# An RWKV6 and MoE kernel on one core: DMA transposes in place of PE transposes for k, r and the MoE input, and a longer lag of the second matmul

## The chip, the cores and the metric

The kernel runs on one core of one Trainium2 chip. The metric is device time in microseconds (us) of one execution. Every timed comparison uses runs of the two kernels on the same chip in the same rounds. A run counts as "slow" when it is more than 1.5% above the fastest run of the same kernel, and ratios use the other, fast runs alone.

The engines are named as in the profile: PE is the matmul engine and PEld its weight loads, DVE, ACT and POOL are the vector, scalar and general-purpose engines, and SP is the engine whose queue starts all DMAs of this kernel.

## The reference

Attention in the RWKV6 form, then a two-layer MoE block with a tanh gelu. Sizes: 4 batches, 8 heads, 768 steps, head width 48; model width 384, hidden width 2048.

```python
def _attn_ref(r, k, v, w, u):            # each [B, H, S, D] = [4, 8, 768, 48]
    state = zeros(B, H, D, D)
    for t in range(S):
        cur = einsum('bhd,bhe->bhde', u * k[t], v[t])
        y[t] = einsum('bhd,bhde->bhe', r[t], state + cur)
        state = w[t][..., None] * state + einsum('bhd,bhe->bhde', k[t], v[t])
    return y

x = attn_out.transpose(0, 2, 1, 3).reshape(B * S, H * D)      # [3072, 384]
h = x @ w_in                                                  # [3072, 2048]
g = 0.5 * h * (1 + tanh(sqrt(2/pi) * (h + 0.044715 * h**3)))
out = g @ w_out                                               # [3072, 384]
```

## The kernel before

The work is cut into 12 units: 3 windows of 256 steps, 4 batches each. A turn of the main loop does the MoE of unit q, the attention matmuls of unit q+1, and the decays and multiplies ("prep") of unit q+2. The matmuls take k and r (already multiplied by decays, called kk and rq) and the attention output x with another axis on the partitions, so the PE transposes them itself, into PSUM (in the trace of before 0.90 us per unit for k and r and 0.33 for x), and DVE copies the result out (0.68 us each for k and r, 0.56 for x).

```python
    # prep(q): products on DVE, one instruction per tensor
    DVE.tensor_tensor(out=kk[:, :, :, 0:D], in0=tdh(kt), in1=dec(e1), op=AL.mult)
    DVE.tensor_tensor(out=rq[:, :, :, 0:D], in0=tdh(rt), in1=dec(fq), op=AL.mult)

    def a2(q, which):                       # transposes of k (0) and r (1)
        src = (kk, rq)[which]
        ps = ps_a.tile([P, G, 2, 2, 64], BF, tag="a", name=f"T{q}_{which}")
        for g in range(G):
            for t2 in range(2):
                PE.transpose(ps[:, g, :, t2, :], src[:, t2, ds(2 * g, 2), :], ident)
        dst = pw2.tile([P, G, 2, 2, 64], BF, tag=f"T{which}", name=f"TT{q}_{which}")
        DVE.tensor_copy(out=dst, in_=ps)

    # a3(q, rnd): the score matmuls "mt", stationary kT = TT_0, moving rT = TT_1
    # a5(q, c2):  y += rT x state on PE, then ACT copies y to xs[:, c2, :]

    def a6(q):                              # transpose of x
        for c2 in range(2):
            for cb in range(NCB):
                PE.transpose(ps[:, cb, c2, :], xs[:, c2, ts(cb, P)], ident)
        DVE.tensor_copy(out=xT, in_=ps.rearrange("p a b t -> p a (b t)"))

    # mm1(q, i): six matmuls into PSUM tile h (two buffers), then one gelu on ACT
    # mm2(q, c2, fts): one matmul per ft into o (c2 is the half of the 256 rows)

    for q in range(NU):
        # ... loads of k, r, v (unit q+3) and w (unit q+4) ...
        table("gelu")                       # ACT table load
        ramp = q < 2                        # ... ramp: all mm1 first ...
        for i in range(8):
            if not ramp:
                mm1(q, i)
            if i >= 2:                      # mm2 lags mm1 by two
                mm2(q, 0, (2 * i - 4, 2 * i - 3))
            if i in (1, 3, 4, 5, 6, 7):
                next(att, None)             # a2 | a3 | a3 | a4 | a5 | a5 of unit q+1
            # ... cumulative sums of unit q+2 at i == 6 ...
        table("exp")                        # ACT table load
        exps(q + 2); ln(q + 3)              # decays, on ACT
        mm2(q, 0, range(12, 16))
        # ... a6(q + 1) ...
        store(q, 0)                         # DVE copy, two DMAs
        prep(q + 2); prep_b(q + 2)
        mm2(q, 1, range(16))
        store(q, 1)
```

## Time and profile before

| | before |
|---|---|
| median (3 runs), us | 235.33 (235.24 to 236.41) |
| span of the profiled run, us | 235.9 |
| granted PE clock, mean | 0.968 |
| period of a unit in the steady part, us | 16.56 |
| first mm1 of unit 2 (third unit) / of unit 11 (last), us | 74.04 / 220.64 |

To see what sets the period of a unit, one boundary between two units has to be read on two engines. This is the PE timeline of before: start, time, engine, line, operation, output and inputs, sizes, number of instructions and, in brackets, an idle time ahead of them with what ended it.

```profile
136.21 0.82 PE L345 MATMUL h_7_2167<-xT_1899,w_in_sb 128*128 128x256 bf16 x6
...
138.10 0.49 PE L329 MATMUL xTp_2196<-ident,xs_2148 128*128 128x128 bf16 x6
138.43 2.76 PE L354 MATMUL o_1_2223<-w_out_sb,g_1948 128*128 128x384 bf16 x16
141.03 0.82 PE L345 MATMUL h_0_2253<-xT_2203,w_in_sb 128*128 128x256 bf16 x6
141.69 0.82 PE L345 MATMUL h_1_2261<-xT_2203,w_in_sb 128*128 128x256 bf16 x6
142.34 0.61 PE L236 MATMUL T_1_2269<-ident,rq_128 128*128 128x128 bf16 x8
142.79 0.61 PE L236 MATMUL T_0_2280<-ident,kk_126 128*128 128x128 bf16 x8
143.75 0.81 PE L345 MATMUL h_2_2291<-xT_2203,w_in_sb 128*128 128x256 bf16 x6 [0.36 <-ACT g_2252 L347]
```

And this is the ACT timeline of before over the same stretch.

```profile
137.06 0.60 ACT L347 ACTIVATE g_1948<-h_7_2167 128x512 bf16<-128x512 f32 x1 [1.75 <-PE h_7_2167 L345]
137.56 0.49 ACT L321 ACTIVATE xs_2148<-y_1_2071 128x384 bf16<-128x384 f32 x1
138.06 1.28 ACT L156 ACT_TABLE_LOAD   x1
...
141.81 1.28 ACT L158 ACT_TABLE_LOAD   x1
143.10 0.60 ACT L347 ACTIVATE g_2252<-h_0_2253 128x512 bf16<-128x512 f32 x1
```

From the last gelu of a unit (137.06) to the first of the next (143.10) ACT has 6.04 us of work without a gap: the copy of xs, two table loads, the decays. The PE has only two PSUM buffers for h, so h_2 can't start before that gelu has read h_0; it waits 0.36 us. Everything that the PE does between h_7 and h_2, the transposes included, therefore lies in the shadow of this ACT chain. A unit is this shadow plus the PE work from h_2 to the end of h_7 (9.67 us).

The stores are the only DMAs of before that are as small as the new transposes. From the SP timeline of before (four stores issued in 4.87 us, some of that waiting for data) and from its list of DMA issues (count, KB each, median us from issue to landing):

```profile
123.12 4.87 SPq L365 DMA_DIRECT2D out_dram<-ob_1901  x4
128.09 0.55 SPq L69 DMA_DIRECT2D k_1939<-in_k_dram  x1
```

```profile
out_dram<-ob_1901 SPq DMA_DIRECT2D x4, 96.0 KB, 2.2
```

The load of k takes SP 0.55 us to issue (those of r, v and w behind it 0.68, 0.86 and 1.17), a store 0.55 to 0.58 where two follow each other without a wait (1.12 and 1.10 us for two); a store lands in 2.2 us from the start of its issue.

### The profile page before, as it was taken

The page shows a single profiled execution, that of the slowest core. Times are in us where ns is not written, and L with a number is a line of the kernel's source. Part 1 is how long each engine was busy: PE and PEld are TensorE (multiplying, and loading weights), DVE is VectorE, ACT ScalarE, POOL GpSimd, SP SyncE. Part 2 cuts the span into 40 slices and gives each one's busy share as a digit, 9 for nine tenths or more (in the row PEclk, how much of TensorE's full clock was granted, in tenths as well). Part 3 has the DMA queues.
Part 4 walks back from the last instruction along what each step waited for, and adds up shares of the span by engine and source line. Part 5 has one row for each costly group of instructions (what it writes and reads, how often), then busy time and mean ns, then how long its engine had stood idle before and what let it go on. Part 6 is the DMA issues. An engine that isn't in the chain of part 4 may idle for free.

```text
span 235.9 us, 5759 instructions
## 1 busy us (share of the span) xinstructions
PE 203.4 (86%) x2448; PEld 143.0 (61%) x2448; DVE 131.3 (56%) x211; ACT 134.0 (57%) x223; POOL 104.5 (44%) x87
## 2 busy tenths in 40 slices
PE   0456787598895999999999999999999999999992
PEld 0334564357564767667767667676777677677761
DVE  7684686561636538547547747656285376374200
ACT  3433780566255449459368377395494684765670
POOL 3473792639008504806708509329158076060000
PEclk9999996779997999999999999999999999999998
DMA  7999999713902911942923914915719120020202
GB/s 173 307 396 297 331 320 255 160 33 72 231 15 54 246 25 36 206 98 53 232 56 75 257 24 111 210 33 124 182 35 212 24 62 10 13 56 0 68 1 67
DMA packets 56969, 30.45 MB, mean 129 GB/s; under 512 B 50928, under 2 KB 56176, under 8 KB 56944
## 3 DMA queue, kind: packets, MB, share of 16 engines
q1 hardware_dynamic: 56944, 30.09, 52.1%
q8 instruction: 19, 0.31, 0.6%
q14 instruction: 6, 0.05, 0.1%
HBM read 25.36 MB, written 4.72 MB: 127 GB/s over the span
## 4 chain that ended last, share of the span: by engine, by line
PE 54%; ACT 19%; DVE 11%; issue 9%; POOL 3%; DMA 2%; DVEq 0%; ACTq 0%; POOLq 0%
ACT L156 5%; DVE w_out_sb L86 2%; DMA w_89<-in_w_dram 2%; PE o_0_532 L354 1%; DVE rq_127 L203 1%; ACT logw_124 L162 1%; PE o_0_3678 L354 1%; PE o_0_3457 L354 1%; PE o_0_3175 L354 1%; PE o_1_3740 L354 1%; PE o_1_3632 L354 1%; PE o_1_3389 L354 1%; POOL rk_418 L210 1%; POOL rk_418 L212 1%; ACT logw_122 L162 1%
## 5 line engine op out<-in xcount | busy, mean ns | idle before, releaser
L345 PEld LDWEIGHTS <-w_in_sb 128*128 128x128 bf16 x576 | 54.0, 99 | 21.1 <-issue 9.9
L156 ACT ACT_TABLE_LOAD x13 | 16.7, 1283 | 0.9 <-PEq L487 0.7
L158 ACT ACT_TABLE_LOAD x12 | 15.4, 1283 | 0.2
L171 PEld LDWEIGHTS <-strict 128*128 128x128 bf16 x24 | 2.5, 104 | 9.9 <-issue 9.5
L215 POOL TENSOR_TENSOR am_997<-blk,al_975 128x384 f32<-128x384 bf16 x2 | 2.4, 1230 | 12.5 <-ACT al_975 L187 12.5
L215 POOL TENSOR_TENSOR am_1304<-blk,al_1273 128x384 f32<-128x384 bf16 x2 | 2.4, 1229 | 11.5 <-ACT al_1273 L187 11.5
L215 POOL TENSOR_TENSOR am_1608<-blk,al_1577 128x384 f32<-128x384 bf16 x2 | 2.4, 1230 | 8.3 <-ACT al_1577 L187 8.3
L215 POOL TENSOR_TENSOR am_1912<-blk,al_1881 128x384 f32<-128x384 bf16 x2 | 2.4, 1230 | 8.3 <-ACT al_1881 L187 8.3
L215 POOL TENSOR_TENSOR am_2216<-blk,al_2185 128x384 f32<-128x384 bf16 x2 | 2.4, 1230 | 8.3 <-ACT al_2185 L187 8.3
L215 POOL TENSOR_TENSOR am_2520<-blk,al_2489 128x384 f32<-128x384 bf16 x2 | 2.4, 1228 | 8.3 <-ACT al_2489 L187 8.3
L215 POOL TENSOR_TENSOR am_2811<-blk,al_2780 128x384 f32<-128x384 bf16 x2 | 2.4, 1228 | 7.9 <-ACT al_2780 L187 7.9
L215 POOL TENSOR_TENSOR am_3100<-blk,al_3069 128x384 f32<-128x384 bf16 x2 | 2.4, 1228 | 7.9 <-ACT al_3069 L187 7.9
L215 POOL TENSOR_TENSOR am_3382<-blk,al_3352 128x384 f32<-128x384 bf16 x2 | 2.4, 1228 | 7.9 <-ACT al_3352 L187 7.9
L354 PE MATMUL o_0_532<-w_out_sb,g_437 128*128 128x384 bf16 x16 | 5.5, 469 | 0.2 <-ACT w_out_sb L84 0.2
L236 PEld LDWEIGHTS <-rq_127 128*128 128x128 bf16 x48 | 3.4, 104 | 3.3 <-DVE rq_127 L203 3.2
L354 PEld LDWEIGHTS <-g_437 128*128 128x128 bf16 x32 | 3.3, 117 | 3.2 <-issue 2.5
L170 PE MATMUL cum_0_201<-logw_122,strict 128*128 128x384 bf16 x1 | 0.5, 479 | 5.4 <-ACT logw_122 L162 5.4
L362 DVE COPY ob_3736<-o_0_3678 128x384 f32<-128x384 f32 x1 | 0.6, 558 | 7.7 <-PE o_0_3678 L354 7.7
L215 POOL TENSOR_TENSOR am_699<-blk,al_677 128x384 f32<-128x384 bf16 x2 | 2.3, 1187 | 4.3 <-ACT al_677 L187 4.3
L354 PEld LDWEIGHTS <-g_3653 128*128 128x128 bf16 x32 | 3.0, 98 | 1.7 <-ACT g_3653 L347 0.4
L238 DVE COPY TT_1_818<-T_1_809 128x1024 bf16<-128x1024 bf16 x1 | 0.7, 692 | 6.0 <-PE T_1_809 L236 6.0
L354 PE MATMUL o_0_3678<-w_out_sb,g_3653 128*128 128x384 bf16 x16 | 3.8, 327 | 0.0
(942 smaller groups left out, 694.2 us busy)
## 6 DMA issues: line engine op xcount, KB each, us to landing
wi_155<-in_moe_w_in_dram SPq DMA_DIRECT2D x1, 512.0 KB, 5.0
wi_157<-in_moe_w_in_dram SPq DMA_DIRECT2D x1, 512.0 KB, 6.0
wi_159<-in_moe_w_in_dram SPq DMA_DIRECT2D x1, 512.0 KB, 6.7
wi_161<-in_moe_w_in_dram SPq DMA_DIRECT2D x1, 512.0 KB, 7.5
wi_163<-in_moe_w_in_dram SPq DMA_DIRECT2D x1, 512.0 KB, 8.7
wi_165<-in_moe_w_in_dram SPq DMA_DIRECT2D x1, 512.0 KB, 9.6
w_89<-in_w_dram SPq DMA_DIRECT2D x1, 384.0 KB, 3.7
k_91<-in_k_dram SPq DMA_DIRECT2D x1, 384.0 KB, 4.7
```

What stands on the lines that cost most here:

```text
L86: eng.tensor_copy(out=out, in_=in_)
L156: ACT.preload_act_table_set(EXP_SET)
L158: ACT.preload_act_table(AF.Gelu_apprx_tanh)
L162: ACT.activation(out=lw[:, :, :, 0:D].rearrange("p t h d -> p h t d"), in_=ld.pop(("w", q)).rearrange("p h (t d) -> p h t d", t=2), func=A ...
L171: PE.matmul(dst[:, 0:HD], s1, lw[:, 1, :, 0:D], start=False, stop=True)
L203: DVE.tensor_tensor(out=rq[:, :, :, 0:D], in0=tdh(rt), in1=dec(fq), op=AL.mult)
L210: POOL.tensor_tensor(out=rk, in0=kt.rearrange("p h (t d) -> p h t d", t=2), in1=rt.rearrange("p h (t d) -> p h t d", t=2), op=AL.mult)
L212: POOL.tensor_tensor(out=rk, in0=rk, in1=u_bc[:, :, None, :].broadcast_to([P, H, 2, D]), op=AL.mult)
L215: POOL.tensor_tensor(out=am[:, c2], in0=blk.rearrange("p g j d -> p g (j d)"), in1=al[:, :, c2][:, :, None].broadcast_to([P, G, 2 * D]), o ...
L236: PE.transpose(ps[:, g, :, t2, :], src[:, t2, ds(2 * g, 2), :], ident)
L345: PE.matmul(h[:, f, :], w_in_sb[:, cb, ts(ft, P)], xT[:, cb, :], start=(f + cb == 0), stop=(cb == NCB - 1), skip_group_check=True)
L354: PE.matmul(st["o", q, c2], g[:, ft, ts(c2, P)], w_out_sb[:, ft, :], start=(ft == 0), stop=(ft == NFT - 1))
```

## The change

Its intent is to take the transposes off the PE, and their copies out of PSUM off DVE, from the third unit on: SP starts DMAs that transpose from SBUF to SBUF. k and r get two each (64 rows of 1024 elements, so that each half has the layout that the matmuls need), x gets one. They are started as soon as kk and rq are multiplied, at the end of a turn of the loop; before transposes the same unit's k and r behind h_1 of the next turn. The multiplies are halved (one per t2) for the new layout; mm2 lags mm1 by four groups in place of two, and the scores move one group earlier. In the ramp, the second unit's x is now transposed ahead of the multiplies on DVE.

```diff
     def a2(q, which):
-        src = (kk, rq)[which]
-        ps = ps_a.tile([P, G, 2, 2, 64], BF, tag="a", name=f"T{q}_{which}")
-        for g in range(G):
-            for t2 in range(2):
-                PE.transpose(ps[:, g, :, t2, :], src[:, t2, ds(2 * g, 2), :], ident)
-        dst = pw2.tile([P, G, 2, 2, 64], BF, tag=f"T{which}", name=f"TT{q}_{which}")
-        DVE.tensor_copy(out=dst, in_=ps)
+        src = (kk_ps, rq_ps)[which][q % 2]
+        dst = pw2.tile([P, 2, G, 2, 64], BF, tag=f"T{which}", name=f"TT{q}_{which}")
+        if q < 2:
+            ...                              # on the PE, as before
+            return
+        for c2 in range(2):
+            SP.dma_start(out=dst[:, c2].rearrange("p g t x -> p (g t) x"),
+                         in_=src[ds(64 * c2, 64)].rearrange("p g t j d -> p (g t j d)"),
+                         transpose=True)
@@ a6
+        if q < 2:
+            ...                              # on the PE, as before
+        else:
+            SP.dma_start(out=xT.rearrange("p a b t -> p (a b) t"),
+                         in_=xs.rearrange("p a c -> p (a c)"), transpose=True)
@@ main loop
-            if i >= 2:
-                mm2(q, 0, (2 * i - 4, 2 * i - 3))
-            if i in (1, 3, 4, 5, 6, 7):
+            if i >= 4:
+                mm2(q, 0, (2 * i - 8, 2 * i - 7))
+            if i in (2, 3, 4, 6, 7):         # a3 | a3 | a4 | a5 | a5
                 next(att, None)
@@ after the loop over i
-        mm2(q, 0, range(12, 16))
-        if not ramp:
-            for _ in att:
-                pass
+        next(att, None)                      # a6, in every unit
+        mm2(q, 0, range(8, 16))
         store(q, 0)
         if q + 2 < NU:
             prep(q + 2)
+            a2(q + 2, 0)
+            a2(q + 2, 1)
             prep_b(q + 2)
# ... cut: layouts of kk, rq, TT and xT, halved multiplies, order of the loads and of the start-up, mm2(q, 1) in one piece
```

More of the change, by code (lines that the diff above doesn't have):

```diff
@@ L126 @@
     logws = [pfix.tile([P, 2, H, 64], BF, name=f"logw{i}") for i in range(3)]
-    kk_ps = [pfix.tile([P, 2, H, 64], BF, name=f"kk{i}") for i in range(2)]
-    rq_ps = [pfix.tile([P, 2, H, 64], BF, name=f"rq{i}") for i in range(2)]
+    kk_ps = [pfix.tile([P, G, 2, 2, 64], BF, name=f"kk{i}") for i in range(2)]
+    rq_ps = [pfix.tile([P, G, 2, 2, 64], BF, name=f"rq{i}") for i in range(2)]
     for t in logws:
@@ L197, in tdh @@
             return ap.rearrange("p h (t d) -> p t h d", t=2)
-        def dec(ap):
-            return ap.rearrange("p t (h d) -> p t h d", h=H)
-        DVE.tensor_tensor(out=kk[:, :, :, 0:D], in0=tdh(kt), in1=dec(e1), op=AL.mult)
-        DVE.tensor_tensor(out=rq[:, :, :, 0:D], in0=tdh(rt), in1=dec(fq), op=AL.mult)
+        for dst, x, dec in ((kk, kt, e1), (rq, rt, fq)):
+            for t2 in range(2):
+                DVE.tensor_tensor(
+                    out=dst[:, :, t2, :, 0:D],
+                    in0=x[:, :, ds(D * t2, D)].rearrange("p (g j) d -> p g j d", j=2),
+                    in1=dec[:, t2, :].rearrange("p (g j d) -> p g j d", g=G, j=2), op=AL.mult)
         vb = pw2.tile([P, 2, H, D], BF, tag="vb", name=f"vb{q}")
@@ L230, in a2 @@
     def a2(q, which):
-        kk, rq, vb, vsc, am = st["pre", q]
-        src = (kk, rq)[which]
-        ps = ps_a.tile([P, G, 2, 2, 64], BF, tag="a", name=f"T{q}_{which}")
-        for g in range(G):
-            for t2 in range(2):
-                PE.transpose(ps[:, g, :, t2, :], src[:, t2, ds(2 * g, 2), :], ident)
-        dst = pw2.tile([P, G, 2, 2, 64], BF, tag=f"T{which}", name=f"TT{q}_{which}")
-        DVE.tensor_copy(out=dst, in_=ps)
+        src = (kk_ps, rq_ps)[which][q % 2]
+        dst = pw2.tile([P, 2, G, 2, 64], BF, tag=f"T{which}", name=f"TT{q}_{which}")
+        if q < 2:
+            ps = ps_a.tile([P, 2, G, 2, 64], BF, tag="a", name=f"T{q}_{which}")
+            for g in range(G):
+                for t2 in range(2):
+                    PE.transpose(ps[:, :, g, t2, :], src[:, g, t2, :, :], ident)
+            DVE.tensor_copy(out=dst, in_=ps)
+            st["T", q, which] = dst
+            return
[3 more added lines that the diff above has]
+                         transpose=True)
         st["T", q, which] = dst
@@ L249, in a3 @@
                         PE.matmul(mts[j][ds(64 * c2, 64), gi, t2, :],
-                                  kT[ds(64 * j, D), g, c2, t2, :],
-                                  rT[ds(64 * j, D), g, c2, :, :],
+                                  kT[ds(64 * j, D), c2, g, t2, :],
+                                  rT[ds(64 * j, D), c2, g, :, :],
                                   start=(gi + t2 == 0), stop=(gi + t2 == 2))
@@ L292, in a4p @@
                     rows = ds(64 * c2, 64)
-                    PE.matmul(p2[c2][:, g, :], kk[rows, t2, ds(2 * g, 2), :],
+                    PE.matmul(p2[c2][:, g, :], kk[rows, g, t2, :, :],
                               vb[rows, t2, ds(2 * g, 2), :],
@@ L315, in a5 @@
             if s is not None:
-                PE.matmul(ys[c2][:, ds(2 * g, 2), :], rT[:, g, c2, :, :], s[:, g, :],
+                PE.matmul(ys[c2][:, ds(2 * g, 2), :], rT[:, c2, g, :, :], s[:, g, :],
                           start=False, stop=True, skip_group_check=True)
@@ L325, in a6 @@
         xs = st.pop(("xs", q))
-        ps = ps_a.tile([P, NCB, 2, P], BF, tag="a", name=f"xTp{q}")
-        for c2 in range(2):
-            for cb in range(NCB):
-                PE.transpose(ps[:, cb, c2, :], xs[:, c2, ts(cb, P)], ident)
-        xT = pw2.tile([P, NCB, WIN], BF, tag="xT", name=f"xT{q}")
-        DVE.tensor_copy(out=xT, in_=ps.rearrange("p a b t -> p a (b t)"))
+        xT = pw2.tile([P, 2, NCB, P], BF, tag="xT", name=f"xT{q}")
+        if q < 2:
+            ps = ps_a.tile([P, 2, NCB, P], BF, tag="a", name=f"xTp{q}")
+            for c2 in range(2):
+                for cb in range(NCB):
+                    PE.transpose(ps[:, c2, cb, :], xs[:, c2, ts(cb, P)], ident)
+            DVE.tensor_copy(out=xT, in_=ps)
+        else:
+            SP.dma_start(out=xT.rearrange("p a b t -> p (a b) t"),
+                         in_=xs.rearrange("p a c -> p (a c)"), transpose=True)
         st["xT", q] = xT
@@ L344, in mm1 @@
             for cb in range(NCB):
-                PE.matmul(h[:, f, :], w_in_sb[:, cb, ts(ft, P)], xT[:, cb, :],
+                PE.matmul(h[:, f, :], w_in_sb[:, cb, ts(ft, P)], xT[:, :, cb, :],
                           start=(f + cb == 0), stop=(cb == NCB - 1), skip_group_check=True)
@@ L371, in attention @@
     def attention(q):
-        a2(q, 1)
-        a2(q, 0)
-        yield
         a3(q, 0)
@@ L387, in attention, with krv @@
         yield
+    def krv(q):
+        if q < NU:
+            for nm in ("k", "r", "v"):
+                load(q, nm)
     for i in range(6):
         load_w_in(i)
-    for nm in ("k", "r", "v"):
-        load(1, nm)
+    table("exp")
+    ln(0)
+    a1(0)
+    exps(0)
+    prep(0)
+    a2(0, 0)
+    a2(0, 1)
+    krv(1)
     for i in range(5):
@@ L398 @@
     load(3, "w")
-    for nm in ("k", "r", "v"):
-        load(2, nm)
-    table("exp")
-    ln(0)
-    a1(0)
-    exps(0)
-    prep(0)
     ln(1)
     att = attention(0)
-    next(att)
     next(att)
@@ L425 @@
     prep(1)
+    a2(1, 0)
+    a2(1, 1)
     prep_b(1)
+    krv(2)
     for q in range(NU):
-        if q + 3 < NU:
-            for nm in ("k", "r", "v"):
-                load(q + 3, nm)
+        krv(q + 3)
         if q + 4 < NU:
@@ L445 @@
                 mm1(q, i)
-            if i >= 2:
-                mm2(q, 0, (2 * i - 4, 2 * i - 3))
-            if i in (1, 3, 4, 5, 6, 7):
+            if i >= 4:
+                mm2(q, 0, (2 * i - 8, 2 * i - 7))
+            if i in (2, 3, 4, 6, 7):
                 next(att, None)
-            if i == 6 and 0 < q and q + 2 < NU:
-                a1(q + 2)
+            if i == 6:
+                if q > 0 and q + 2 < NU:
+                    a1(q + 2)
         table("exp")
@@ L466 @@
             prep(q + 2)
+            a2(q + 2, 0)
+            a2(q + 2, 1)
             prep_b(q + 2)
-        mm2(q, 1, range(8))
-        for _ in att:
-            pass
-        mm2(q, 1, range(8, 16))
+        mm2(q, 1, range(16))
         store(q, 1)
```

## The prediction

Its sum comes to 229 us. The 2.2 us to landing are those of the stores.

> **What bounds the kernel now.** From the third unit on a unit takes 16.56 us (first mm1 of successive units in the PE timeline: 107.91, 124.47, 141.03 us); the windows view has the PE 16.33 of 17 us busy. But the PE's order is tied to a chain on ACT: its timeline has 6.04 us without a gap from the last gelu of a unit (120.50) to the first of the next (126.54): gelu, xs copy, table load 1.28, exps, ln 0.88, table load 1.28. mm1 h_2 needs the PSUM buffer that this first gelu empties, and waits 0.36 us for it. So period = last gelu to h_2, 6.7 us (137.06 to 143.75) + PE work from h_2 to the end of h_7 (9.67) + 0.2.
>
> **What the change does.** Per unit the PE loses the sixteen k/r transposes (0.90 us) and the six of x (0.33); DVE loses copies of 0.69 + 0.68 + 0.56 us. But these 1.23 us of PE lie outside the h_2-to-h_7 stretch, in the shadow of the ACT chain: their removal mostly turns into a longer wait of h_2 (about 0.9 us). What shortens the period is the mm2 lag: six mm2 matmuls instead of ten lie between h_2 and h_7, 4 x 0.163 = 0.65 us. Best case 15.9 us per unit.
>
> **The new wait.** SP gets five transposes per unit in its in-order queue. x: xs is ready 1.0 us after the last gelu starts, the next mm1 needs it 4.3 to 5.3 us after; two stores of 96 KB landed in 2.2 us (DMA issue list): this fits. k and r: the multiplies end about 3.9 and 5.0 us after the last gelu. Four DMAs, issued at 0.65 us each as the stores are, start at 4.0 to 6.0; with 2.2 us to landing the last is there at about 8.0. The first score matmul (a3) wants it at about 7.4. So I expect 0.3 to 0.9 us of waiting on TT, which eats most of the 0.65. [...] If issuing one takes 1.5 us of SP, the kernel is some 10% slower: the main risk.
>
> **Ramp.** Surer: mm1 of the second unit waits 1.06 us for xT and the third 2.37 (DVE does k and r first), T copies and transposes there cost another 2 us, and x of the second unit is now transposed before the multiplies. The first mm1 comes later (unit 1's transposes go first and wait for a 2.56 us multiply), which the w_out casts hide. Net 3 to 5 us.
>
> **Sum.** Ramp -4, nine units at -0.2 (-0.6 to +1.0 or worse): 229 us; 8 in 10 between 219 and 250. Faster by over 2%: 0.54; within 2%: 0.20; slower by over 2%: 0.26.
>
> **What shows it.** Period 16.3 us; h_2 waiting for ACT 0.5 to 1 us; the score matmul waiting for DMA TT under 1 us; no wait of h_0 for xT; PE busy down by 10 to 13 us; transposes landing in 2 to 2.5 us, SP issue under 0.8 us.
>
> **What would make it wrong.** Transposes of 4 us or more, slow SP issue, or loads in flight delaying them: then TT or xT is the longest wait and periods exceed 17 us. Or landing in under 1.5 us: 15.9 us and 224 us.

## More of the kernel before

From the page of the profile of before: the span, the busy time of each engine, and the granted PE clock in 40 slices of the span (in tenths, 9 is 90% or more).

```profile
span 235.9 us, 5759 instructions
...
PE 203.4 (86%) x2448; PEld 143.0 (61%) x2448; DVE 131.3 (56%) x211; ACT 134.0 (57%) x223; POOL 104.5 (44%) x87
...
PEclk9999996779997999999999999999999999999998
```

The PE is the busiest engine (86% of the span), and from 77.62 us on, just behind the ramp, its clock stays up (1.00 until 234.64).

## The result and the profile after

| | before | after |
|---|---|---|
| median of the same rounds (4 runs each), us | 235.87 (235.24 to 238.91) | 270.75 (268.87 to 271.82) |
| ratio to before, 95% interval | 1 | 1.148 (1.139 to 1.157) |
| span of the profiled run, us | 235.9 | 269.1 |
| granted PE clock, mean | 0.968 | 0.879 |
| period of a unit in the steady part, us | 16.56 | 20.76 |
| first mm1 of unit 2 / of unit 11, us | 74.04 / 220.64 | 69.53 / 253.76 |

A ratio here is the mean time of one kernel's fast runs over that of the other's of the same rounds, so it is not quite the ratio of the medians; the slow 238.91 of before is in its median here and not in the ratio.

The change made the kernel about 15% slower. The starts of the first mm1 say where: the ramp is 4.5 us shorter (69.53 in place of 74.04), the nine units from there to unit 11 take 184.2 us in place of 146.6, which is 37.6 more or 4.2 per unit, and the end after unit 11's first mm1 is the same 15.3 us. That sums to 33.1 us, and the spans differ by 33.2.

The page of after, the same lines as of before, and the chain of work that ended last, by engine:

```profile
span 269.1 us, 5404 instructions
...
PE 207.2 (77%) x2228; PEld 139.4 (52%) x2228; DVE 117.6 (44%) x205; ACT 134.0 (50%) x223; POOL 98.8 (37%) x87
...
PEclk9999975799959959989959968988998968968999
...
PE 47%; ACT 18%; DMA 18%; SPq 8%; issue 5%; DVE 2%; POOL 0%; ACTq 0%
```

Two things stand out. A quarter of the final chain is now DMA and SP's queue (18% and 8%; in before DMA had 2% and SP's queue did not appear). Not all of that is the transposes: 5 of the 8% are issues of loads (SPq L69 in the page's split by line). And the PE is busy for longer (207.2 us) although it has 220 instructions fewer, while the clock now dips in every unit.

One boundary between units, on the PE timeline of after:

```profile
126.13 0.82 PE L356 MATMUL h_7_1786<-xT_1528,w_in_sb 128*128 128x256 bf16 x6
...
128.58 2.76 PE L365 MATMUL o_1_1847<-w_out_sb,g_1593 128*128 128x384 bf16 x16
131.18 0.82 PE L356 MATMUL h_0_1877<-xT_1811,w_in_sb 128*128 128x256 bf16 x6
...
133.67 0.81 PE L356 MATMUL h_2_1893<-xT_1811,w_in_sb 128*128 128x256 bf16 x6 [1.02 <-ACT g_1876 L358]
136.26 0.26 PE L256 MATMUL mt_0_0_1901<-TT_1_1842,TT_0_1839 48*64 48x128 bf16 x1 [1.77 <-DMA TT_1_1842<-rq_127]
137.58 0.26 PE L256 MATMUL mt_0_0_1901<-TT_1_1842,TT_0_1839 48*64 48x128 bf16 x1 [1.06 <-DMA TT_1_1842<-rq_127]
...
138.15 1.46 PE L356 MATMUL h_3_1922<-xT_1811,w_in_sb 128*128 128x256 bf16 x6
...
140.12 1.46 PE L356 MATMUL h_4_1951<-xT_1811,w_in_sb 128*128 128x256 bf16 x6
```

The last gelu of this unit started on ACT at 126.98. The scores (mt) begin 10.6 us after that, at 137.58, after two waits for the transpose of r, 1.77 and 1.06 us. The first of the two ends when the first half of r is there; one matmul runs, and the next needs the second half. After that h_3 and h_4 take 1.46 us where h_0 to h_2 take 0.82: the same six matmuls at half the clock.

What SP did meanwhile, on its timeline in after (the second column is the time from the first issue of the group to the end of the last), and the landing time of the transposes of r from the list of DMA issues:

```profile
127.99 1.21 SPq L341 DMA_TRANSPOSE xT_1811<-xs_1767  x1
129.36 1.12 SPq L376 DMA_DIRECT2D out_dram<-ob_1821  x2
130.86 2.53 SPq L243 DMA_TRANSPOSE TT_0_1839<-kk_125  x2
133.49 2.52 SPq L243 DMA_TRANSPOSE TT_1_1842<-rq_127  x2
```

```profile
TT_1_1842<-rq_127 SPq DMA_TRANSPOSE x2, 2.8
```

On DVE, kk was complete at 130.83 and rq at 132.40. SP starts on kk at once, but it takes 2.53 us for two issues, and reaches rq at 133.49, 1.1 us after rq was ready. The second half of rq is issued at about 134.75 and lands 2.8 us later, at 137.55. That is the wait of the PE, to within 0.03 us.

The busy time and the clock around this, in stretches of 2 us of after (stretch, length, busy us and instruction count of PE, PEld, DVE, ACT, POOL, then the granted clock, the DMA share and GB/s):

```profile
132.00:134.00 2.00, 0.98 (x10) 0.72 (x8) 1.73 (x3) 1.99 (x3) 1.75 (x2) 1.00 0.71 110
134.00:136.00 2.00, 0.49 (x5) 0.30 (x3) 0.00 (x0) 0.71 (x2) 2.00 (x3) 0.91 0.58 87
136.00:138.00 2.00, 0.68 (x16) 0.52 (x15) 0.00 (x0) 0.00 (x0) 1.92 (x2) 0.50 0.68 119
...
140.00:142.00 2.00, 2.00 (x16) 1.04 (x8) 1.29 (x2) 0.63 (x2) 0.00 (x0) 0.50 1.15 275
```

The mean of 0.91 from 134 to 136 puts the drop to 0.50 at about 135.64 (0.36 us at half clock), and the clock stays there until 142.47. The gap between h_2 and the scores is 3.09 us, from 134.49 to 137.58, interrupted by a single matmul. In windows of 0.1 us over the whole of after, all its changes of the clock lie a whole number of steps of 3.41 us apart: those at 94.69, 101.51, 118.58, 121.99, 135.64, 142.47 and 156.12, for example, are 2, 5, 1, 4, 2 and 4 steps apart. So the 3.41 us ahead of a change are looked at here. Those before 142.47, where the clock comes back, are busy throughout. When the clock falls at 135.64, the PE has been idle for only 1.15 us, and the 3.41 us before hold 1.24 us of PE work (h_1 and h_2) and two waits, of 1.02 and 1.15 us. So the clock falls inside the wait for the scores and not at its end.

### The profile page after: what moved, and what is told of

It is laid out like the page before. It is cut to its first block, busy times and chain, and to the rows that moved or that the text cites. A ratio compares the mean times of both kernels' runs of the same rounds, so it can differ in the third digit from the quotient of the medians.

```text
span 269.1 us, 5404 instructions
## 1 busy us (share of the span) xinstructions
PE 207.2 (77%) x2228; PEld 139.4 (52%) x2228; DVE 117.6 (44%) x205; ACT 134.0 (50%) x223; POOL 98.8 (37%) x87
## 4 chain that ended last, share of the span: by engine, by line
PE 47%; ACT 18%; DMA 18%; SPq 8%; issue 5%; DVE 2%; POOL 0%; ACTq 0%
SPq L69 5%; ACT L156 4%; DMA wi_163<-in_moe_w_in_dram 3%; DMA k_454<-in_k_dram 2%; DMA TT_1_3207<-rq_128 1%; DMA xT_2647<-xs_2603 1%; SPq L243 1%; ACT L158 1%; ACT logw_124 L162 1%; DMA TT_1_2408<-rq_127 1%; DMA TT_1_2946<-rq_127 1%; DMA TT_1_999<-rq_128 1%; DMA TT_1_1276<-rq_127 1%; DMA TT_1_722<-rq_127 1%; DMA TT_1_2125<-rq_128 1%
## 5 line engine op out<-in xcount | busy, mean ns | idle before, releaser
L356 PEld LDWEIGHTS <-w_in_sb 128*128 128x128 bf16 x576 | 56.7, 104 | 26.3 <-issue 14.2
L156 ACT ACT_TABLE_LOAD x13 | 16.7, 1283 | 0.9 <-PEq L497 0.7
L216 POOL TENSOR_TENSOR am_3199<-blk,al_3170 128x384 f32<-128x384 bf16 x2 | 2.0, 1031 | 12.7 <-ACT al_3170 L187 12.7
L216 POOL TENSOR_TENSOR am_1268<-blk,al_1238 128x384 f32<-128x384 bf16 x2 | 2.0, 1031 | 12.6 <-ACT al_1238 L187 12.6
L216 POOL TENSOR_TENSOR am_1551<-blk,al_1521 128x384 f32<-128x384 bf16 x2 | 2.0, 1033 | 12.6 <-ACT al_1521 L187 12.6
L216 POOL TENSOR_TENSOR am_2117<-blk,al_2087 128x384 f32<-128x384 bf16 x2 | 2.0, 1033 | 12.6 <-ACT al_2087 L187 12.6
L216 POOL TENSOR_TENSOR am_2400<-blk,al_2370 128x384 f32<-128x384 bf16 x2 | 2.0, 1030 | 12.5 <-ACT al_2370 L187 12.5
L216 POOL TENSOR_TENSOR am_2670<-blk,al_2640 128x384 f32<-128x384 bf16 x2 | 2.0, 1030 | 11.9 <-ACT al_2640 L187 11.9
L216 POOL TENSOR_TENSOR am_2938<-blk,al_2908 128x384 f32<-128x384 bf16 x2 | 2.0, 1032 | 11.9 <-ACT al_2908 L187 11.9
L216 POOL TENSOR_TENSOR am_1834<-blk,al_1804 128x384 f32<-128x384 bf16 x2 | 2.0, 1031 | 11.9 <-ACT al_1804 L187 11.9
L216 POOL TENSOR_TENSOR am_991<-blk,al_961 128x384 f32<-128x384 bf16 x2 | 2.0, 1030 | 9.9 <-ACT al_961 L187 9.9
L365 PEld LDWEIGHTS <-g_463 128*128 128x128 bf16 x32 | 3.7, 122 | 3.3 <-issue 2.2
L365 PE MATMUL o_0_578<-w_out_sb,g_463 128*128 128x384 bf16 x16 | 5.4, 501 | 0.0
L256 PE MATMUL mt_0_0_3258<-TT_1_3207,TT_0_3204 48*64 48x128 bf16 x8 | 0.8, 297 | 4.7 <-DMA TT_1_3207<-rq_128 4.7
L365 PEld LDWEIGHTS <-g_2442 128*128 128x128 bf16 x32 | 3.2, 101 | 1.6
L365 PEld LDWEIGHTS <-g_1876 128*128 128x128 bf16 x32 | 3.2, 101 | 1.6
L365 PEld LDWEIGHTS <-g_1033 128*128 128x128 bf16 x32 | 3.2, 101 | 1.6
L365 PEld LDWEIGHTS <-g_1310 128*128 128x128 bf16 x32 | 3.2, 101 | 1.6
L365 PEld LDWEIGHTS <-g_2159 128*128 128x128 bf16 x32 | 3.2, 101 | 1.6
```

The costliest lines, as they stand in the source:

```text
L156: ACT.preload_act_table_set(EXP_SET)
L216: POOL.tensor_tensor(out=am[:, c2], in0=blk.rearrange("p g j d -> p g (j d)"), in1=al[:, :, c2][:, :, None].broadcast_to([P, G, 2 * D]), o ...
L256: PE.matmul(mts[j][ds(64 * c2, 64), gi, t2, :], kT[ds(64 * j, D), c2, g, t2, :], rT[ds(64 * j, D), c2, g, :, :], start=(gi + t2 == 0), sto ...
L356: PE.matmul(h[:, f, :], w_in_sb[:, cb, ts(ft, P)], xT[:, :, cb, :], start=(f + cb == 0), stop=(cb == NCB - 1), skip_group_check=True)
L365: PE.matmul(st["o", q, c2], g[:, ft, ts(c2, P)], w_out_sb[:, ft, :], start=(ft == 0), stop=(ft == NFT - 1))
```

## The experiments

The expectations call the theories by letters. **A**: each transpose takes SP a fixed time of about 1.25 us to issue, whatever its size, so five of them in one in-order queue come too late. **B**, the rival: the cost goes with the bytes and their transfer. **C**: a share of the loss is the lowered clock, which follows from the wait. **D**: the new order of the work, without any DMA, is already worse. Eleven kernels ran; all gave correct results.

### one128: one transpose of 128 rows for each of k and r

```diff
-        for c2 in range(2):
-            SP.dma_start(out=dst[:, c2]..., in_=src[ds(64 * c2, 64)]..., transpose=True)
+        SP.dma_start(out=dst.rearrange("p g t c x -> p (g t) (c x)"),
+                     in_=src.rearrange("p g t j d -> p (g t j d)"), transpose=True)
@@ a5: the two halves of rT are no longer contiguous, so each matmul is cut in two
-                PE.matmul(ys[c2][:, ds(2 * g, 2), :], rT[:, c2, g, :, :], s[:, g, :], ...)
+                for t in range(2):
+                    PE.matmul(ys[c2][ds(64 * t, 64), ds(2 * g, 2), :], rT[:, g, t, c2, :],
+                              s[:, g, :], ...)
```

> One transpose of 128 rows each for k and r instead of two of 64 rows (same bytes, half the issues; a5 uses two half-width matmuls per group because of the layout). Theory A (each transpose occupies the SP queue for a fixed 1.24 us whatever its size, and that serial time makes TT late): one issue stays at about 1.25 us, the last TT lands some 2.3 us earlier, the PE gap before the scores falls from 3.2 to about 1 us and the clock no longer drops; period 20.76 to about 17.0 us, time 234 to 242 us. Theory B (the data itself is slow: issue and landing go with the bytes): issue about 2.5 us each, landing about 4 us, time stays at 265 to 272 us.

Measured: 241.71 us in the one fast run, whose profile is read here; three others, at 245.36, 245.81 and 249.18, were slow by the rule above, so no interval is given. Before had 235.20 to 238.24 in these rounds. Those four give a median of 245.58, a little above the range expected; the fast run is inside. The SP timeline of one128:

```profile
173.91 1.26 SPq L242 DMA_TRANSPOSE TT<-kk  x1
175.52 1.23 SPq L242 DMA_TRANSPOSE TT<-rq  x1
```

A transpose with twice the rows is still issued in 1.23 to 1.26 us (single ones took up to 1.38). Its landing takes 3.1 (r) to 3.3 us (k) in place of 2.8. The scores begin 8.7 us after the last gelu (169.91 to 178.62) in place of 10.6, and the units are 16.9 to 18.7 us apart, 17.4 on average. So the issue time is per instruction, as A has it.

### split4: four transposes of 32 rows for each of k and r

```diff
-        for c2 in range(2):
-            SP.dma_start(out=dst[:, c2]..., in_=src[ds(64 * c2, 64)]..., transpose=True)
+        for c4 in range(4):
+            c2, hh = c4 // 2, c4 % 2
+            SP.dma_start(out=dst[:, c2]...[:, :, ds(32 * hh, 32)],
+                         in_=src[ds(32 * c4, 32)]..., transpose=True)
```

> Four transposes of 32 rows each for k and r instead of two (same bytes, twice the issues). Theory A (fixed SP time per transpose): four more issues of 1.24 us per unit, period about 25 to 26 us, time 305 to 325 us. Theory B (bytes): issue falls to about 0.62 us, time stays within 265 to 275 us.

Measured: 320.96 us (319.40 and 322.52), ratio 1.357 (1.343 to 1.370); the same bytes, and 50 us more than after. The SP timeline of split4:

```profile
150.67 5.09 SPq L244 DMA_TRANSPOSE TT<-kk  x4
155.87 5.07 SPq L244 DMA_TRANSPOSE TT<-rq  x4
```

Again 1.27 us each, for half the bytes, with landing in 2.4 us. Four issues more per unit cost about 5 us of period (21 to about 26). B is refuted for the issue, and nearly so for the landing: 32, 64 and 128 rows land in 2.4, 2.8 and 3.1 to 3.3 us, so four times the bytes add under 1 us.

### fill10: ten mm2 matmuls held back and run while the transposes are awaited

The waiting is left in, but the PE is given work in it: ten of the sixteen mm2 matmuls of the second half are done behind h_2 of the next unit.

```diff
+            if i == 2 and q > 2:
+                mm2(q - 1, 1, range(6, 16))
+                store(q - 1, 1)
             if i in (2, 3, 4, 6, 7):
                 next(att, None)
@@ end of the unit
-        mm2(q, 1, range(16))
-        store(q, 1)
+        mm2(q, 1, range(6))          # from the third unit on
```

> As after, but ten of the sixteen second-half mm2 matmuls of a unit are held back and run just before the score matmuls of the next unit, where TT is awaited; DMA and SP work unchanged. Theory C (part of the loss is the PE clock, which drops to half after the 3.2 us gap): gaps stay under 2 us each, PEclk stays near 1.0, h_3 and h_4 take 0.82 instead of 1.46 us, period about 19.2 us, time 254 to 260 us. If the lateness of TT alone counts and the low clock only fills time that would be waited anyway: 266 to 271 us.

Measured: 260.23 us (259.04 to 262.91), ratio 1.102 (1.092 to 1.113), just above the range. On its PE timeline the scores still begin 10.57 us after the last gelu (160.63 to 171.20), but h_3 runs at full speed. The second fence is one of its stretches of 2 us: right behind the wait the clock is 1.00.

```profile
167.97 1.79 PE L365 MATMUL o<-w_out_sb,g 128*128 128x384 bf16 x10
169.90 0.21 PE L256 MATMUL mt<-TT,TT 48*64 48x128 bf16 x1
171.20 0.41 PE L256 MATMUL mt<-TT,TT 48*64 48x128 bf16 x15 [1.09 <-DMA TT<-rq]
171.55 0.83 PE L356 MATMUL h<-xT,w_in_sb 128*128 128x256 bf16 x6
```

```profile
172.00:174.00 2.00, 2.00 (x48) 1.31 (x45) 2.00 (x4) 1.07 (x2) 0.89 (x1) 1.00 1.25 305
```

From the scores to the next last gelu it takes 8.19 us, where the unit of after that was read above takes 10.16 for the same work. The period is 18.76. The difference, 10.16 - 8.19 = 1.97 us, is the clock's part in that unit, nearly half of its 4.2. Not every unit of after loses as much: between the gelu table loads of units 2 and 11 after takes 181.8 us and fill10 169.9, which is 1.3 us per unit on average (fill10's first unit there, which the edit leaves as it was, is hardly shortened: 20.2 us against 20.8). C is shown, with a size of 1.3 us per unit on average and 2.0 in the unit read.

### all_pe, x_dma_only and kr_dma_only: the new order with fewer or no DMA transposes

In all_pe the new order and layouts stay, but all transposes are on the PE (those of k and r behind mm1 1 of the next turn, as in before).

```diff
-        if q < 2:                    # in a2 and a6
+        if True:
@@ main loop
+            if i == 1 and 0 < q and q + 1 < NU:
+                a2(q + 1, 1)
+                a2(q + 1, 0)
@@ behind prep(q + 2)
-            a2(q + 2, 0)
-            a2(q + 2, 1)
```

> The new schedule, ramp and layouts, lag of four, but every transpose on the PE (k and r at the place where before has them). If the transposing DMAs alone cause the loss, as theories A and B say: 224 to 232 us, h_2 the main wait, period about 16.2 us, ramp gain of 4.5 us kept. Rival D (the greater mm2 lag leaves the PE without work to fill waits and is itself the loss): 245 us or more.

Measured: 243.16 us (240.20 to 243.48), ratio 1.025 (1.017 to 1.033): a miss. A gain was expected if D was false, and there is a loss, though under the 245 that D was to show; the order without the DMA is a little worse, and explains a small share of the 15% at most. The period is 17.37 us. The DVE timeline of all_pe shows why:

```profile
138.14 0.56 DVE L373 COPY ob<-o 128x384 f32<-128x384 f32 x1 [0.74 <-PE o L365]
138.62 1.02 DVE L201 TENSOR_TENSOR kk<-k,e 128x384 bf16<-128x384 f32 x2
139.55 2.29 DVE L201 TENSOR_TENSOR rq<-r,fq 128x384 bf16<-128x384 f32 x2
...
143.09 1.27 DVE L239 COPY TT<-T 128x1024 bf16<-128x1024 bf16 x2
```

The multiply of r takes 2.29 us in two halves, where before does it whole in 0.95. In all_pe, POOL had started its own multiply (am) at 139.36, ahead of it; in before the two start together (141.14 on DVE, 141.15 on POOL), r keeps its 0.95 us and POOL's pair takes 2.42 in place of 2.07. Each half of r ends 0.41 to 0.42 us after the POOL instruction that had started ahead of it (140.74 after 140.32, 141.84 after 141.43): the two go together in this trace, and no run shows why. So the copies that free the scores come at 143.09, and the scores wait 0.85 us for DVE, 9.1 us after the last gelu. With more mm2 behind the last gelu the DVE chain (output copy, multiplies, copies) has become the limit.

In x_dma_only x alone goes by DMA, otherwise as all_pe:

```diff
# against all_pe, in a6
-        if True:
+        if q < 2:                    # x by one DMA transpose from the third unit on
```

> As all_pe (243 us, period 17.37 us), but x by DMA. In all_pe the chain of a unit runs through DVE: copy of x, copy of the output, k and r multiplies, T copies, scores. Without the transposes of x on the PE and their DVE copy the output copy and the multiplies start about 0.4 to 0.9 us earlier: period 16.5 to 17.0 us, time 234 to 240 us; xT lands 3.8 us after the last gelu, before h_0 asks for it. If the DMA of x were itself late: 245 us or more.

Measured: 231.90 us (231.79 to 234.25), ratio 0.982 (0.975 to 0.988), better than expected; period 16.22. In kr_dma_only k and r go by DMA, otherwise as after:

```diff
# against after, in a6
-        if q < 2:
+        if True:                     # x on the PE in every unit
```

> As after, but x is transposed by the PE in every unit; k and r still by four DMAs. If k and r carry the whole loss through the SP queue (theory A): period stays 20.5 to 21 us, time 266 to 274 us. If the transpose of x, first in the queue, carries a part: 3 us or more below 270.

Measured: 279.59 us (279.48 and 279.70), ratio 1.181 (1.171 to 1.191), slower than expected and slower than after; the scores begin 11.4 us after the last gelu (150.88 to 162.30). Both comparisons agree: x by DMA is a gain (1.025 to 0.982 without the k and r transposes, 1.181 to 1.148 with them), and the whole loss comes with the four transposes of k and r. In kr_dma_only the PE's x transpose and its copy also delay the DVE chain that feeds those four: the first of them is issued 4.7 us after the last gelu (155.56), in place of 3.9.

### lag2: after, with the old lag and later scores

```diff
-            if i >= 4:
-                mm2(q, 0, (2 * i - 8, 2 * i - 7))
-            if i in (2, 3, 4, 6, 7):
+            if i >= 2:
+                mm2(q, 0, (2 * i - 4, 2 * i - 3))
+            if i in ((3, 4, 5, 6, 7) if q >= 2 else (2, 3, 4, 6, 7)):
@@
-        mm2(q, 0, range(8, 16))
+        mm2(q, 0, range(12, 16))
```

> As after, all its DMA transposes kept, but mm2 lags by two as in before and, from the third unit on, the scores run one step later (after h_3, with four mm2 matmuls ahead of them). TT still lands 10.6 us after the last gelu (theory A). By theory A plus clock, the PE gap before the scores falls from 3.2 to about 1.8 us, the clock holds, and h_3 has left the stretch behind the scores (8.19 - 0.66 us): period about 18.1 us, time 244 to 250 us. If the lag is no part of the loss: 266 us or more.

Measured: 257.87 us (255.02 to 258.79), ratio 1.091 (1.083 to 1.098); a miss, by some 8 us. Setting the scores one group later and giving the PE four mm2 matmuls back in the stretch takes 13 us off after's time (ratio 1.148 to 1.091), so the longer lag and the early scores, which this run does not separate, did harm in company with the late transposes. But the clock still fell to 0.50 in some units; in one of them (the fall is at 133.37) the gaps of the PE around it are 1.39, 0.46 and 1.12 us. In fill10 the clock held, with gaps of 1.10, 1.38 and 1.09 us per unit. The idle total of a window does not separate the two either: the 3.41 us before that fall in lag2 (129.96 to 133.37 in the windows view) hold 1.83 us of PE work, while a stretch of the same length in fill10 (107.30 to 110.71) holds only 1.47 and the clock is still 1.00 in the next 3.41 us. (Both stretches end where a change could be seen: in fill10 the clock changes at 42.45, 45.86, 49.27, 76.58 and 79.99, all multiples of 3.41 us apart, and 110.71 is ten such steps after 76.58.) What sets the fall stays open.

### y_x_lag4, y_x_lag2, y_lag4_pe: the good parts on top of before

These start from before, so k and r are transposed on the PE in before's order and layout, and the multiplies are whole.

```diff
# y_x_lag4 against before
@@ a6
+        if q < 2:
+            ...                      # on the PE, as before
+        else:
+            SP.dma_start(out=xT.rearrange("p a b t -> p (a b) t"),
+                         in_=xs.rearrange("p a c -> p (a c)"), transpose=True)
@@ main loop
-            if i >= 2:
-                mm2(q, 0, (2 * i - 4, 2 * i - 3))
+            if i >= 4:
+                mm2(q, 0, (2 * i - 8, 2 * i - 7))
@@ after the loop over i
-        mm2(q, 0, range(12, 16))
-        if not ramp:
-            for _ in att:
-                pass
+        for _ in att:                # a6 ahead of the multiplies in the ramp too
+            pass
+        mm2(q, 0, range(8, 16))
```

> The kernel before, with its whole multiplies, k and r on the PE after h_1 and scores after h_3; changed are x by DMA from the third unit on, a lag of four, and the transposes of x ahead of the multiplies in the first units too. SP gets one transpose per unit, which fits. The ACT chain with h_2 stays 6.7 us, the stretch from h_2 to h_7 has six mm2 matmuls instead of ten (9.0 instead of 9.67 us): period 15.9 to 16.2 us, ramp 2 to 4 us shorter, time 226 to 231 us. If h_0 waits for xT or the DVE chain decides as in all_pe: 235 us or more.

Measured: 228.49 us (227.67 to 228.91, 6 runs), ratio 0.9645 (0.960 to 0.969), period 15.90. y_x_lag2 is the same with before's lag of 2, y_lag4_pe the same with x on the PE:

```diff
# y_x_lag2 against y_x_lag4
-            if i >= 4:
-                mm2(q, 0, (2 * i - 8, 2 * i - 7))
+            if i >= 2:
+                mm2(q, 0, (2 * i - 4, 2 * i - 3))
-        mm2(q, 0, range(8, 16))
+        mm2(q, 0, range(12, 16))
# y_lag4_pe against y_x_lag4: a6 as in before
```

> As y_x_lag4 (228.5 us, period 15.90 us), but the lag is two as in the kernel before, so ten mm2 matmuls lie between h_2 and h_7. If taking the transposes of x off the PE gains nothing per unit by itself, because the PE only waits longer for the first gelu at h_2: period 16.5 to 16.6 us as before, h_2 waits about 0.7 us, only the ramp gain remains: 231 to 234 us. If the PE time taken away counts directly: period 16.2 us or less, 228 us or less.

> As y_x_lag4, but x transposed on the PE in every unit: the lag of four alone. The PE has then about 7.2 us of work and waiting for xs between the last gelu and h_2, more than the 6.7 us of the ACT chain, so part of the 0.65 us that the lag moves comes back: period 16.2 to 16.6 us, time 231 to 235 us. If the lag alone brings the gain: 15.9 us, 227 to 230 us.

Measured: y_x_lag2 232.57 us (232.01 to 232.81), ratio 0.982 (0.975 to 0.988); unit 2's first mm1 is at 69.79, 4.3 us earlier than in before, which is nearly all of the gain, and most units are 16.2 to 16.7 us apart, as in before. y_lag4_pe 236.86 us (236.19 to 237.30), ratio 1.000 (0.995 to 1.006), slower than expected: its PE waits 0.58 us for xs at the transposes of x, with the mm2 work that stood in front of them now behind them. Here the two parts need each other. x by DMA alone frees PE time that lies in the shadow of the ACT chain and gains nothing per unit; the lag alone moves mm2 into that shadow until the shadow is longer than the ACT chain; together they give 0.66 us per unit.

### y_k_lag5: k by one DMA transpose as well

```diff
# against y_x_lag4
@@ a2, for k from the third unit on (one transpose of 128 rows)
+                SP.dma_start(out=dst.rearrange("p t g c x -> p (t g) (c x)"),
+                             in_=src.rearrange("p t h d -> p (t h d)"), transpose=True)
@@ main loop
-            if i >= 4:
-                mm2(q, 0, (2 * i - 8, 2 * i - 7))
+            if i >= 5:
+                mm2(q, 0, (2 * i - 10, 2 * i - 9))
@@ behind prep(q + 2)
+            a2(q + 2, 0)
```

> As y_x_lag4, and k too by DMA, in one transpose of 128 rows, with a lag of five. One issue of 1.25 us starts when k's multiply ends, 4.2 us after the last gelu, and lands 3.3 us after its start, at about 7.5, before the scores ask for it at 8.1; so two transposes per unit still fit where five did not. Four mm2 matmuls are left between h_2 and h_7: period 15.5 to 15.7 us, time 224 to 228 us. If it lands too late after all: 229 us or more, with the scores waiting for DMA.

Measured: 227.18 us (227.04 to 227.97, 6 runs), ratio 0.960 (0.955 to 0.965), the fastest median, and faster than before and after. Its lead over y_x_lag4 (0.6% in the medians, from other rounds, with overlapping intervals) is not clear of the noise. Its SP and PE timelines:

```profile
131.13 1.23 SPq L347 DMA_TRANSPOSE xT<-xs  x1
...
134.30 1.26 SPq L242 DMA_TRANSPOSE TT<-kk  x1
```

```profile
136.81 1.47 PE L362 MATMUL h<-xT,w_in_sb 128*128 128x256 bf16 x12 [0.25 <-ACT g L364]
138.21 0.42 PE L262 MATMUL mt<-TT,TT 48*64 48x128 bf16 x16
```

k is issued at 134.30 and lands 3.1 us later, at 137.4; the scores start at 138.21 and don't wait for it. Two transposes per unit fit into the time that the ACT chain leaves, where five didn't. Ordered by the transposes in SP's queue, whole kernels have these periods: one (y_x_lag4) 15.9 us, two (y_k_lag5) about 15.6, three (one128) about 17.4, five (after) 20.76, nine (split4) about 26. These kernels differ in order and lag too, so the row shows a trend and not a slope; kr_dma_only, with four and its x on the PE, has about 21.5 and lies outside it, and lag2 and fill10, with five, have about 19.

## Why the prediction was wrong

The predicted 229 us (219 to 250) and the measured 270.75 differ by some 42 us. In the steady part a period of 16.3 was predicted and 20.76 measured.

**Right: what bounds before.** The 1.23 us of transposes on the PE lie in the shadow of the ACT chain, as predicted. h_2 waits 1.02 us for ACT in after (predicted 0.5 to 1), and y_x_lag2 shows that taking x's 0.33 us off the PE alone gains nothing per unit.

**Right: the lag.** The 0.65 us per unit that the lag was to give is there when nothing is in the way: y_x_lag4 has a period of 15.90 against 16.56, and the best case was put at 15.9.

**Right in size: the ramp.** 4.5 us shorter (predicted 3 to 5), and 4.3 in y_x_lag2, but 2.2 in y_x_lag4 (first mm1 of unit 2 at 71.89). The parts that the prediction lists were not traced one by one.

**Right: x.** x's transpose was said to fit. Issued at 127.99 and landed 2.8 us later, at 130.8, it is there before h_0 at 131.18. The slowest, xT_2647, took 3.45 us and landed at 193.0, just as h_0 started (193.03); h_2 of that unit still waited for ACT (0.71 us), so that cost nothing.

**Wrong, and the step that failed: "Four DMAs, issued at 0.65 us each as the stores are, start at 4.0 to 6.0; with 2.2 us to landing the last is there at about 8.0."** The multiplies end at 3.9 and 5.4 us after the last gelu, close to the 3.9 and 5.0 given. But a transpose is issued in 1.25 us and not in 0.65, so the last of the four starts 7.8 us after the last gelu in place of 6.0 (1.8 us late), and lands in 2.8 us and not in 2.2 (0.6 us more): 10.6 us in place of the 8.2 that these terms add up to (the prediction says about 8.0). Landing is counted from the start of the issue, and from its end a transpose takes 1.5 us (136.02 to 137.54) and a store 1.6, so by this reckoning the 0.6 too is the longer issue. The size of an issue was carried over from another kind of DMA, and even for stores the trace of before has 0.55 to 0.58. one128 and split4 show that it is a fixed time per transpose: 1.23 to 1.27 us in the fences here for 32, 64 and 128 rows. The prediction named "slow SP issue" as its main risk and put it at 10% for 1.5 us; the error was to give 0.65 as the centre with nothing of this kind in the trace. The bytes mattered least: from 64 to 128 rows they double from 128 to 256 KB, and landing grows by only 0.3 to 0.5 us (from 2.8 to 3.1 and 3.3).

**Not foreseen: the clock.** The waits leave the PE 2.17 us idle in the 3.41 us before 135.64, and then it runs at half clock for 6.8 us. fill10, which fills the gap and leaves the wait, sizes it at 2.0 us in the unit that was read, and at 1.3 on average. For the same reason PE busy time rose by 3.8 us where a fall of 10 to 13 was predicted: fewer instructions, but slower ones. Nothing of this was in the prediction, whose wait was 0.3 to 0.9 us; in after the longest single idle stretch of the unit read is 1.77 us.

The terms of that unit close: 10.6 us to the scores, 8.19 from there to the next last gelu at full clock, 1.97 for the lowered clock, 20.76 in all. Against the prediction, which had 8.0 to the scores and about 8.3 behind them, the period grew by 2.6 (late transposes: 1.8 of issue, 0.6 of landing and 0.2 of its own rounding) and by about 1.9 behind the scores, where the clock's part in this unit was sized at 1.97.

**What stays open.** Why the clock fell in lag2 and not in fill10. Why single transposes took SP about twice as long (one of x 2.28 us in one128, where the others took about 1.22; one of r 2.37 us in after). And whether issuing from a second queue would take the 1.25 us off the path: that was not tried.

## What to carry to other kernels

Before moving work to DMA, count the instructions that one queue has to issue between the time when the data is ready and the time when it is wanted, and measure the issue time of just that kind of DMA: here five transposes of 1.25 us each didn't fit and two did, in kernels whose order differs too. Freed time of the busiest engine gained nothing per unit here as long as it lay in the shadow of another chain (0.33 us of x in y_x_lag2); a second part (here the lag) had to move work into it (15.90 us per unit in place of 16.56 in y_x_lag4). When a change adds waits on the PE, look at the clock too, even where no single wait is long: here the clock fell to 0.50 behind a wait of 1.02 us and the first 1.15 us of the next.
